# Third chunk's values first in the first batch, and squares of 32 for q and k from the sixteenth head pair

## Chip, cores and metric

The kernel runs on one core of a Trainium2 chip. The metric is device time in microseconds (us) of one launch. The kernel before was run three times: median 1395.97 us, from 1393.84 to 1398.77.

## The reference

Attention with RMS-normed queries and keys, and then a two-layer network over all heads of a token. Everything is float32 but the two weight matrices, which are handed over in float64 as pairs of 32-bit words.

```python
# q, k, v: (batch 8, heads 12, seq 448, head_dim 64); g_q, g_k: (64,)
rmsnorm(x, g) = x / sqrt(mean(x * x, axis=-1) + 1e-6) * g
scores = rmsnorm(q, g_q) @ rmsnorm(k, g_k).T / sqrt(64)
attn   = softmax(scores)                       # over the keys
x      = (attn @ v) as (8 * 448 = 3584, 768)   # heads side by side
h      = x @ w_in                              # (768, 2048)
g      = h - tanh(h)
out    = g @ w_out                             # (2048, 768)
```

## The kernel before

**Steps and slots.** Work is cut into 48 steps; step s is one batch b = s // 6 and one pair of its heads, s % 6 (NP = 6 pairs to a batch). The attention of a batch runs ahead of the network of the batch before it. The order of all instructions is written out by hand: each engine does them in the order in which the program names them, and a loop calls one function per step, a slot.

- `first_slot(s)`, s = -3 to 5: batch 0. No network work exists yet; what runs beside attention is the rounding of the float64 weights to float32 (`weight`, L290, with `round_weight_a` on ScalarE L71/L72, `round_weight_b` on VectorE L78/L82, `round_weight_c` on POOL L90) and sums of weight blocks (`combine`, L322, on VectorE).
- `early_slot(s)`, s = 6 to 11: attention of batch 1 beside the network of batch 0 (`hidden`, `project_first`), with the rest of the weights still being loaded (L265, L269) and rounded.
- `slot(s)`, s = 12 to 47: attention of batch 2 and later beside the network of the batch before. Weight blocks now come from a ring (L386, L388).

`run(gap)` (the matmuls of `stream`) puts so many ns of the network's matmuls at its place. From s = 13 (FOLDED) `slot` goes through `visit`, which mixes values and the next pair's scores.

**Attention of one pair.** The 448 keys are three chunks of 128 (c = 0, 1, 2) and a last one of 64 (KF = 3). `scores(s, c)` makes eight small matmuls (32 keys each, L506; the profile counts two instructions for each of them) and two exponentials on ScalarE (L512), into `p` for chunks 0 and 1, `p_full` for chunk 2, `p_last` for the rest. `p` and `p_last` have two buffers, `p_full` has one:

```python
name, bufs = ("p", 2) if c < 2 else ("p_full", 1) if c < KF else ("p_last", 2)
```

so the scores of pair s+1, chunk 2, can be made at once, but their exponential has to wait until the values of pair s have read `p_full`. `values(s, av)` (L598) multiplies the three chunks with v, 24 matmuls (48 instructions in the profile, L605), twelve for each half n of the queries; its loop has n outside and c inside, 0, 1, 2. `totals` (L611) sums the probabilities on TensorE and VectorE takes the reciprocal (L631); `divide` (L665) scales the values. In `first_slot` the order at the end is: the last chunk's scores of s+1, `last_values`, `values`, scores of s+1 chunk 2, `norm_q(s + 3)`, `divide`, `weight`, `combine`.

**Two ways to prepare q and k.** Pairs 0 to 17 are loaded with rows on partitions (q as 112 partitions with four rows each, k as three chunks of 128 rows with three neighbouring rows to a partition). ScalarE squares them (L123, L124), VectorE sums (L133, L134), POOL takes the power -0.5 (L135), the q rows are scaled in `norm_q` (L410, on VectorE; for pairs 9 to 14 eight ScalarE multiplications instead, the `if` at the head of `norm_q`), and `turn` (L416) transposes them on TensorE, four for k (L421), four for q (L425), with the copies to `kT` and `qT` on ScalarE (L423, L429). From pair 18 on (batch FIRST = 3), `by_blocks` is true: `load_blocks` brings q and k with eight transfers in squares of 32x32, `square_blocks` (ScalarE L451), `norm_blocks` (VectorE L458 to L462, POOL L463) and `scale_blocks` (VectorE L470) norm them, and `turn_blocks` transposes the squares on VectorE (L480, L484), with kT's scale on ScalarE (L485). No TensorE instruction is needed.

The row order of a batch has to be the same everywhere: with `turn`, the queries come out in an order that depends on how many rows a partition holds, and `store` (L822) puts them right with a strided VectorE transpose (L828) for b < FIRST, a contiguous one otherwise. For the same reason v is loaded row by row in order (`in_order` in `fetch`) for batches from FIRST.

**Queues.** All loads and stores go through SP's queue, in program order; a transfer that waits holds all behind it. The weight loads wait until POOL's L90 has freed their place. An issue also waits for the eighth transfer before it, since eight semaphores take turns.

**PSUM.** Eight banks, five "sc" and three "mm", go round in their groups; in `slot` three "sc" remain and two become `av`. A group of network products that starts (`p` 1, 5, 6 or 4 of `products`, L733) needs an "mm" bank that VectorE or ScalarE has emptied: L789 for example adds the bank of product 5 to s1.

Of the kernel before, what the change touches and what calls it, by code (L numbers as in the profile page):

```python
# [20 lines left out]
NCH = 4  # L21
# [71 lines left out]
def fetch(nc, name, t, pair, in_order=False):  # L93

    S = pair.shape[1]
    P = 128
    KF, KR = S // P, S % P
    if name == "q":
        nc.sync.dma_start(
            out=t.rearrange("p h c d -> p h (c d)"), in_=pair.rearrange("h (p c) d -> p h (c d)", c=NCH)  # L100
        )
        return
    full, rest = pair[:, : KF * P].rearrange("h (p c) d -> h p c d", c=KF), pair[:, KF * P :]
    if name == "v":
        last = t[:, :, KF]
    if in_order:
        for h in range(2):
            nc.sync.dma_start(out=t[:, h, :KF], in_=pair[h, : KF * P].rearrange("(c p) d -> p c d", p=P))
    elif name == "v":
        nc.sync.dma_start(  # L110
            out=t[:, :, :KF].rearrange("p h c d -> p h (c d)"), in_=full.rearrange("h p c d -> p h (c d)")
        )
    else:
        last = t[:, KF]
        for h in range(2):
            nc.sync.dma_start(out=t[:, :KF, h], in_=full[h])
    for r in range(2):
        nc.sync.dma_start(out=last[r * KR : (r + 1) * KR], in_=rest.rearrange("h p d -> p h d"))
# [19 lines left out]
def bounded_path(tc, ctx, q, k, v, moe_w_in, moe_w_out, out, g_col, ident, ones, half_ones, neg_half, early):  # L138
# [17 lines left out]
    nc = tc.nc  # L156
    B, H, S, D = q.shape
    DFF, DM = moe_w_out.shape
    P = 128
    CP = S // NCH  # L160
    NP = H // 2
# [7 lines left out]
    HS = S // 2  # L169
# [4 lines left out]
    BL = 32  # L174
    KF, KR = S // P, S % P
# [27 lines left out]
    def mm_bank():  # L203
        return bank_of("mm")

    loaded = {}

    def load(s, names):
        b, hp = steps[s]
        for name in names:  # L210
            src = {"q": q, "k": k, "v": v}[name]
            if s == 0 and name != "v":
                t = early[name]
            else:
                shape = [CP, 2, NCH, D] if name == "q" else [P, NCH, 2, D] if name == "k" else [P, 2, NCH, D]
                t = nat.tile(shape, F32, name=f"{name}_nat", bufs=3 if name == "v" else 2)
                fetch(nc, name, t, src[b, 2 * hp : 2 * hp + 2], by_blocks(s))
            loaded[name, s] = t


# [210 lines left out]

    FIRST, NJ = 3, S // BL

    def by_blocks(s):
        return has(s) and steps[s][0] >= FIRST

    def load_blocks(s):
# [49 lines left out]
    def sc_bank():  # L489
        return bank_of("sc")  # L490

    def scores(s, c, apart=False):

        rr, kT, qT = turned[s]
        n = S if c < KF else HS
        name, bufs = ("p", 2) if c < 2 else ("p_full", 1) if c < KF else ("p_last", 2)
        if c == 1:
            p = probs[s, 1] = probs[s, 0]
        else:
            p = probs[s, c] = pp.tile([P, 2, 2 if c < 2 else 1, n], F32, name=name, bufs=bufs)  # L500
        tiles = [sc_bank() for _ in range(2)]

        def score(h, i):
            at, first = (i * BL, 0) if c < KF else (i * BL % KR, i * BL // KR * n)
            r = slice(h * D, (h + 1) * D)
            nc.tensor.matmul(  # L506
                tiles[h][i * BL : (i + 1) * BL, :n], lhsT=kT[r, c * P + at : c * P + at + BL],
                rhs=qT[r, first : first + n], start=True, stop=True,
            )

        def exp(h):
            nc.scalar.activation(  # L512
                p[:, h, c if c < 2 else 0, :], tiles[h][:, :n], AF.Exp,
                scale=1.0 if rr is None else rr[:, 0, 2 * c + h : 2 * c + h + 1],
            )

        if apart:
            return [(lambda i, h=h: score(h, i), lambda h=h: exp(h)) for h in range(2)]
        for i in range(P // BL):
            for h in range(2):  # L520
                score(h, i)
        for h in range(2):
            exp(h)

    def full(s):

        return probs[s, 0][:, :, 0], probs[s, 1][:, :, 1], probs[s, 2][:, :, 0]
# [67 lines left out]
        if has(s + 1):  # L595
            scores(s + 1, 2)

    def values(s, av):  # L598
        v_nat, p = loaded.pop(("v", s)), full(s)
        for n in range(2):  # L600
            for c in range(KF):
                for m in range(2):
                    for h in range(2):
                        r = (2 * m + h) * BL
                        nc.tensor.matmul(  # L605
                            av[n][r : r + BL, :HS], lhsT=v_nat[:, h, c, m * BL : (m + 1) * BL],
                            rhs=p[c][:, h, n * HS : (n + 1) * HS], start=False, stop=(c == KF - 1),
                        )
        return av

    def totals(s, dn):  # L611
# [328 lines left out]
    def has(s):  # L940
        return 0 <= s < NS

    def first_slot(s):

        if has(s + 1):
            scores(s + 1, 0)
            scores(s + 1, 1)
        if has(s + 2):
            turn(s + 2, mm_bank(), sc_bank())
        if s > -3:  # L950
            load(s + 4, "qk")
        if s > -3:
            squares(s + 3)
        norm(s + 3)
        if has(s):
            totals(s, mm_bank())
        if has(s + 2):
            load(s + 2, "v")
        if has(s + 1):
            scores(s + 1, KF)  # L960
        if has(s):
            av = [mm_bank() for _ in range(2)]
            last_values(s, av)
            values(s, av)
        if has(s + 1):
            scores(s + 1, 2)
            add(s + 1)
            add_last(s + 1)
        norm_q(s + 3)
        if s == -3:  # L970
            early["g_col"]()
        if has(s):
            divide(s, av)
        weight(EARLY * (s + 3) // (NP + 2))
        combine(2)

    def early_slot(s):
        gap = gap_ns(s)
        totals(s, sc_bank())
        if has(s + 1):  # L980
            scores(s + 1, 0)
            scores(s + 1, 1)
        if has(s + 2):
            load(s + 2, "v")
        run(gap)
        if has(s + 2):
            turn(s + 2, sc_bank(), sc_bank())
        if has(s + 3):
            squares(s + 3)
        if has(s + 4):  # L990
            load(s + 4, "qk")
        run(gap)
        if has(s + 1):
            scores(s + 1, KF)
        av = [sc_bank() for _ in range(2)]
        last_values(s, av)
        divide(s, values(s, av))
        if has(s + 1):
            scores(s + 1, 2)
        for work, n in ((add, 1), (add_last, 1), (norm, 3), (norm_q, 3)):  # L1000
            run(gap / 2)
            if has(s + n):
                work(s + n)

    def slot(s):

        gap = gap_ns(s)
        av = av_banks
        if has(s + 1):
            scores(s + 1, KF)  # L1010
        if s < FOLDED:
            last_values(s, av)
            totals(s, sc_bank())
            divide(s, values(s, av))
            for c in range(KF):
                scores(s + 1, c)
        else:
            visit(s, av)
        if has(s + 2):
            load(s + 2, "v")  # L1020
        if by_blocks(s + 3):
            load_blocks(s + 3)
        blocks = by_blocks(s + 2)
        run(gap / 2)
        if has(s + 1):
            add(s + 1)
        if blocks:
            square_blocks(s + 2)
        run(gap / 2)
        if blocks:  # L1030
            norm_blocks(s + 2)
        elif has(s + 2):
            turn(s + 2, sc_bank(), sc_bank())
        ahead = has(s + 3) and not by_blocks(s + 3)
        if ahead:
            squares(s + 3)
        if has(s + 4) and not by_blocks(s + 4):
            load(s + 4, "qk")
        run(gap / 2)
        folded = has(s + 1) and s + 1 >= FOLDED  # L1040
        if has(s + 1):
            add_last(s + 1)
        if folded:
            fold(s + 1)
        run(gap / 2)
        if blocks:
            scale_blocks(s + 2)
        if ahead:
            norm(s + 3)
        if folded:  # L1050
            gather(s + 1, 0)
        run(gap / 2)
        if blocks:
            turn_blocks(s + 2, 0)
        if folded:
            gather(s + 1, 1)
        run(gap / 2)
        if blocks:
            turn_blocks(s + 2, 1)
        if ahead:  # L1060
            norm_q(s + 3)
        run(gap / 2)
        if folded:
            spread_sums(s + 1)
        run(gap / 2)
# [358 lines left out]
```

## Time and profile before

One profiled execution took 1397.86 us, 1.89 above the median of the three runs; its span, from first to last instruction, is 1396.1.

| engine | busy, us | share of span | instructions |
|---|---|---|---|
| TensorE, matmul (PE) | 1360.6 | 97% | 11864 |
| TensorE, weight load (PEld) | 1133.3 | 81% | 11864 |
| VectorE (DVE) | 940.3 | 67% | 1530 |
| ScalarE (ACT) | 507.9 | 36% | 1153 |
| GpSimd (POOL) | 555.4 | 40% | 348 |

By stage (us; the first two columns are where the stage begins and how long it lasts):

| stage | begins | length | PE busy | DVE busy | ACT busy | POOL busy | clock | DMA share |
|---|---|---|---|---|---|---|---|---|
| start, pairs prepared | 0 | 27.40 | 16.82 | 10.51 | 17.17 | 12.14 | 0.94 | 0.76 |
| batch 0, `first_slot` | 27.40 | 71.50 | 65.32 | 63.27 | 50.70 | 42.52 | 0.98 | 0.77 |
| `early_slot` | 98.90 | 197.76 | 188.16 | 163.18 | 96.24 | 95.93 | 0.97 | 0.79 |
| slots 12 to 15 | 296.66 | 110.60 | 110.60 | 72.39 | 44.51 | 39.49 | 1.00 | 0.55 |
| slots 16 to the end | 407.26 | 988.84 | 979.72 | 630.94 | 299.25 | 365.31 | 1.00 | 0.61 |

How to read it: PE is busy when a matmul runs, so 97% is an upper bound of how well it is used; the clock is the share of full speed that the chip granted TensorE; the DMA share is the mean over 16 DMA engines. The page counts 355,273 DMA packets, 250.01 MB in all (179 GB/s), of which 266,484 packets are under 512 bytes. A name such as L733 is the line of the kernel; a record "x48" is 48 instructions of one line in a row. In a slot with `turn` the page's groups show four transposes of k (273 ns each, L421) and four of q (259 ns, L425).

### The profile page before, as it was taken

What the parts mean: (1) busy time and instruction counts of PE and PEld (TensorE: products, weight loads), DVE (VectorE), ACT (ScalarE), POOL (GpSimd) and SP (SyncE); (2) the same over time, 40 slices, a digit from 0 to 9 for tenths busy, and PEclk for the clock granted to TensorE, in tenths of its full rate; (3) what the DMA queues carried; (4) which work ended last, traced back from release to release, by engine and by line L of the source; (5) the groups of instructions that cost most, each with busy time, mean ns of one, the idle gap of its engine ahead of it and who ended that gap; (6) DMA issues with size and microseconds to landing.
All of it is one profiled execution on the core that took longest, in us unless ns stands there. A gap on an engine that the chain in (4) does not pass through costs nothing.

```text
span 1396.1 us, 29929 instructions
## 1 busy us (share of the span) xinstructions
PE 1360.6 (97%) x11864; PEld 1133.3 (81%) x11864; DVE 940.3 (67%) x1530; ACT 507.9 (36%) x1153; POOL 555.4 (40%) x348
## 2 busy tenths in 40 slices
PE   6999899999999999999999999999999999999997
PEld 2468664478899898889889988988988998899997
DVE  3999888757756688567867668656885677632311
ACT  5866554234423433233332333224333243301100
POOL 4665555224432347224544245423462255402310
PEclk9999999999999999999999999999999999999999
DMA  7769788765556756666656666666556656366663
GB/s 177 175 189 245 244 253 214 207 198 166 158 142 192 182 163 182 170 155 193 181 148 176 195 156 184 184 156 176 171 166 176 172 179 192 100 189 183 192 192 89
DMA packets 355273, 250.01 MB, mean 179 GB/s; under 512 B 266484, under 2 KB 297396, under 8 KB 355124
## 3 DMA queue, kind: packets, MB, share of 16 engines
q1 hardware_dynamic: 355120, 248.00, 63.8%
q8 instruction: 96, 1.57, 0.5%
q14 instruction: 53, 0.43, 0.1%
q10 hardware_dynamic: 4, 0.00, 0.0%
HBM read 214.50 MB, written 33.42 MB: 178 GB/s over the span
## 4 chain that ended last, share of the span: by engine, by line
PE 87%; DVE 5%; DMA 3%; ACT 2%; SPq 1%; issue 1%; POOL 0%; DVEq 0%; ACTq 0%
PE mm L733 65%; PE sc L506 9%; PE sc L567 6%; PE mm L898 4%; PE sc L555 1%; DMA q_nat<-in_q_dram 1%; PE sc L605 1%; DMA w_raw<-in_moe_w_out_dram 1%; DMA w_f<-w_out 1%; DMA w_raw<-in_moe_w_in_dram 1%; DVE w_out L82 1%; PE mm L605 1%; DVE w_out L78 0%; DVE rs L631 0%; ACT p L512 0%
## 5 line engine op out<-in xcount | busy, mean ns | idle before, releaser
L733 PE MATMUL mm<-xT,w_f 128*128 128x224 f32 x1392 | 278.2, 354 | 1.4 <-DVE s L789 1.4
L733 PEld LDWEIGHTS mm<-xT,w_f 128*128 128x128 f32 x1392 | 261.3, 190 | 15.0 <-issue 10.2
L733 PEld LDWEIGHTS mm<-gT,w_f 128*128 128x128 f32 x1344 | 252.8, 190 | 12.8 <-issue 12.8
L733 PE MATMUL mm<-gT,w_f 128*128 128x224 f32 x1344 | 263.0, 354 | 0.0
L506 PE MATMUL sc<-qT,kT 64*32 64x448 f32 (+1 forms) x3072 | 219.1, 505 | 12.8 <-ACT p_last L512 9.4
L463 POOL TENSOR_TENSOR rr_mine<-rr_mine,neg_half 128x28 f32<-128x28 f32 x30 | 145.1, 4835 | 203.3 <-DVE rr_mine L462 203.3
L733 PE MATMUL mm<-tt,w_f 128*128 128x224 f32 x1044 | 208.7, 353 | 0.0
L733 PEld LDWEIGHTS mm<-tt,w_f 128*128 128x128 f32 x1044 | 197.0, 190 | 4.4 <-issue 4.4
L733 PE MATMUL mm<-tg,w_f 128*128 128x224 f32 x1008 | 197.7, 353 | 0.0
L770 POOL TENSOR_TENSOR gT<-s,th 128x448 f32<-128x448 f32 x96 | 118.6, 1245 | 188.1 <-ACT th L769 181.6
L733 PEld LDWEIGHTS mm<-tg,w_f 128*128 128x128 f32 x1008 | 190.6, 190 | 0.0
L506 PEld LDWEIGHTS sc<-qT,kT 64*32 64x32 f32 x3072 | 72.3, 107 | 84.3 <-issue 58.8
L671 DVE TENSOR_TENSOR xT<-xT,sc 128x448 f32<-128x448 f32 x35 | 21.7, 621 | 163.3 <-PE sc L506 118.5
L693 POOL TENSOR_TENSOR tt<-xT,tt 128x224 f32<-128x224 f32 x23 | 31.4, 1366 | 240.5 <-DVE xT L675 217.5
L650 ACT COPY sum_g<-sum 32x14 f32<-32x14 f32 x280 | 56.2, 201 | 180.8 <-DVE sum L642 175.0
L567 PE MATMUL sc<-p,v_nat 64*32 64x448 f32 x1120 | 110.5, 536 | 0.0
L769 ACT ACTIVATE th<-s 128x448 f32<-128x448 f32 x96 | 55.3, 576 | 114.4 <-DVE s L795 57.2
L135 POOL TENSOR_TENSOR rr<-rr,neg_half 112x8 f32<-112x8 f32 (+1 forms) x36 | 59.6, 1676 | 61.5 <-DVE rr L134 37.4
L512 ACT ACTIVATE p<-sc 128x448 f32<-128x448 f32 x120 | 65.2, 543 | 46.8 <-PE sc L506 34.5
L898 PE MATMUL mm<-gT,w_out 128*128 128x448 f32 x192 | 76.8, 556 | 0.3 <-POOL w_out L90 0.3
L898 PEld LDWEIGHTS mm<-gT,w_out 128*128 128x128 f32 x192 | 36.6, 195 | 39.3 <-issue 37.2
L567 PEld LDWEIGHTS sc<-p,v_nat 64*32 64x32 f32 x1120 | 40.6, 107 | 31.1 <-issue 31.1
(151 smaller groups left out, 1853.1 us busy)
## 6 DMA issues: line engine op xcount, KB each, us to landing
w_f<-w_in SPq DMA_DIRECT2D x196, 384.0 KB, 3.3
w_f<-w_out SPq DMA_DIRECT2D x147, 512.0 KB, 3.8
w_raw<-in_moe_w_out_dram SPq DMA_DIRECT2D x16, 768.0 KB, 5.0
out_dram<-th SPq DMA_DIRECT2D x192, 56.0 KB, 1.9
w_in<-w_out SPq DMA_DIRECT2D x21, 384.0 KB, 6.7
qk_nat<-in_q_dram SPq DMA_DIRECT2D x120, 56.0 KB, 2.3
qk_nat<-in_k_dram SPq DMA_DIRECT2D x120, 56.0 KB, 2.4
gT<-in_moe_w_in_dram SPq DMA_DIRECT2D x32, 192.0 KB, 4.2
```

The source lines that it names most:

```text
L135: nc.gpsimd.tensor_tensor(out=r, in0=r, in1=neg_half[:rows], op=ALU.pow)
L463: nc.gpsimd.tensor_tensor(out=mine, in0=mine, in1=neg_half[:, :1].to_broadcast([P, 2 * NJ]), op=ALU.pow)
L506: nc.tensor.matmul(tiles[h][i * BL : (i + 1) * BL, :n], lhsT=kT[r, c * P + at : c * P + at + BL], rhs=qT[r, first : first + n], start=True ...
L512: nc.scalar.activation(p[:, h, c if c < 2 else 0, :], tiles[h][:, :n], AF.Exp, scale=1.0 if rr is None else rr[:, 0, 2 * c + h : 2 * c + h ...
L567: nc.tensor.matmul(av[g][i * BL : (i + 1) * BL, :S], lhsT=v_nat[keys, h, c, m * BL : (m + 1) * BL], rhs=p[keys, h], start=first, stop=True ...
L605: nc.tensor.matmul(av[n][r : r + BL, :HS], lhsT=v_nat[:, h, c, m * BL : (m + 1) * BL], rhs=p[c][:, h, n * HS : (n + 1) * HS], start=False, ...
L650: nc.scalar.copy(out=acc[h * BL : (h + 1) * BL, g], in_=part[g * BL : (g + 1) * BL, h * NJ : (h + 1) * NJ])
L693: eng.tensor_tensor(out=t2, in0=x22, in1=t1, op=ALU.subtract)
L733: nc.tensor.matmul(bank[:, f * HS : (f + 1) * HS], lhsT=w[:, c * width + f, :], rhs=moving[p](c), start=(first and f == 0 and c == 0), sto ...
L769: nc.scalar.activation(th, h, AF.Tanh, bias=0.0, scale=1.0)
L770: eng.tensor_tensor(out=g[:, rows, cols], in0=h, in1=th, op=ALU.subtract)
L898: nc.tensor.matmul(bank[:, :S], lhsT=w_out_row(f, n // HC)[:, n % HC * P : (n % HC + 1) * P], rhs=g[:, f, :], start=(f == 0), stop=(f == C ...
```

## The change

Two edits. In the first batch's slots, `values` is cut in two: the values of chunk 2 for both halves of the queries come first, then chunk 2's scores of the next pair, then the values of chunks 0 and 1. `values` now has the chunk outside and the half inside wherever it is called (slots 0 to 12).

And the squares of 32 begin three pairs earlier, with pair 15 instead of 18, which is in the middle of batch 2. Since a batch can have one row order only, FIRST becomes 2: batch 2's pairs 12 to 14, which still go through `turn`, are loaded with rows in order too (`fetch` gets this for q, two transfers, and for k), v of pairs 12 to 17 is, and `store` transposes batch 2 contiguously. The eight transfers for pair 15 are issued late in slot 12, those for 16 and later at their usual place at the slot's start.

```diff
@@ fetch
     if name == "q":
+        if in_order:
+            for h in range(2):
+                nc.sync.dma_start(out=t[:, h], in_=pair[h].rearrange("(c p) d -> p c d", c=NCH))
+            return
...
     if name == "v":
         last = t[:, :, KF]
+    elif in_order:
+        last = t[:, KF]
     if in_order:
         for h in range(2):
-            nc.sync.dma_start(out=t[:, h, :KF], in_=pair[h, : KF * P].rearrange("(c p) d -> p c d", p=P))
+            to = t[:, h, :KF] if name == "v" else t[:, :KF, h]
+            nc.sync.dma_start(out=to, in_=pair[h, : KF * P].rearrange("(c p) d -> p c d", p=P))
@@ load
-                fetch(nc, name, t, src[b, 2 * hp : 2 * hp + 2], by_blocks(s))
+                fetch(nc, name, t, src[b, 2 * hp : 2 * hp + 2], in_order(s))
@@
-    FIRST, NJ = 3, S // BL
+    FIRST, NJ = 2, S // BL
+    TURNED = 2 * NP + 3
 
     def by_blocks(s):
+        return has(s) and s >= TURNED
+
+    def in_order(s):
         return has(s) and steps[s][0] >= FIRST
@@
-    def values(s, av):
-        v_nat, p = loaded.pop(("v", s)), full(s)
-        for n in range(2):
-            for c in range(KF):
+    def values(s, av, chunks=(2, 0, 1)):
+        v_nat, p = loaded["v", s], full(s)
+        for c in chunks:
+            for n in range(2):
...
-                            rhs=p[c][:, h, n * HS : (n + 1) * HS], start=False, stop=(c == KF - 1),
+                            rhs=p[c][:, h, n * HS : (n + 1) * HS], start=False, stop=(c == 1),
...
+        if 1 in chunks:
+            del loaded["v", s]
         return av
@@ first_slot
             last_values(s, av)
-            values(s, av)
+            values(s, av, (2,))
         if has(s + 1):
             scores(s + 1, 2)
+        if has(s):
+            values(s, av, (0, 1))
+        if has(s + 1):
             add(s + 1)
             add_last(s + 1)
@@ early_slot
-        if has(s + 4):
+        if has(s + 4) and not by_blocks(s + 4):
             load(s + 4, "qk")
@@ slot
-        if by_blocks(s + 3):
+        if by_blocks(s + 3) and s + 3 > TURNED:
             load_blocks(s + 3)
...
         if blocks:
             turn_blocks(s + 2, 1)
+        if s + 3 == TURNED:
+            load_blocks(s + 3)
         if ahead:
             norm_q(s + 3)
```

## The prediction

> **What bounds the kernel now.** I read the page first: its chain of waits (the first line under part 4) is TensorE almost throughout.
>
> ```profile
> PE 87%; DVE 5%; DMA 3%; ACT 2%; SPq 1%; issue 1%; POOL 0%; DVEq 0%; ACTq 0%
> ```
>
> So an edit pays only where it takes TensorE instructions away, or where TensorE waits. The change touches three stretches; I took them one at a time.
>
> First batch (about 27 to 99 us). The chain in order of time seems to say that ScalarE and TensorE take turns: the values, the third chunk's scores, then the exponential of p_full.
>
> ```profile
> 49.10 2.41 PE mm L605 x48
> 51.51 1.02 PE sc L506 x16
> 52.53 0.04 issue
> 52.57 0.71 ACT p_full L512 x2
> ```
>
> That is what the first edit attacks. But the timelines of VectorE, POOL and SP over the same slots show what the next slot really starts from (start, duration, engine; in brackets the idle time before and its releaser):
>
> ```profile
> 39.73 1.87 POOL L90 TENSOR_TENSOR w_out<-w_out,gT 128x768 int32<-128x768 int32 x1 [3.44 <-ACT n L123]
> ...
> 41.63 1.74 SPq L265 DMA_DIRECT2D gT<-in_moe_w_in_dram  x4
> 43.47 0.37 SPq L99 DMA_DIRECT2D q_nat<-in_q_dram  x1
> 43.95 1.24 SPq L116 DMA_DIRECT2D k_nat<-in_k_dram  x2
> 45.24 1.28 SPq L118 DMA_DIRECT2D k_nat<-in_k_dram  x2
> ...
> 50.13 0.63 ACT L124 ACTIVATE sq<-k_nat 128x512 f32<-128x512 f32 x1 [0.71 <-DMA k_nat<-in_k_dram]
> ...
> 50.79 0.69 DVE L133 TENSOR_REDUCE rr<-sq 128x8 f32<-128x512 f32 x1 [0.40 <-ACT sq L124]
> ```
>
> SP holds q and k behind a weight load that waits for POOL's L90 (41.60); k lands at 50.13, and only then can VectorE sum its squares. From there VectorE does not rest until 98.9; the stretches table (columns: length, busy of PE, PEld, DVE, ACT, POOL, clock, DMA share, GB/s) has
>
> ```profile
> 53.73:98.90 45.17, 41.32 (x607) 25.42 (x592) 43.93 (x61) 32.53 (x58) 28.73 (x20) 0.96 0.79 210
> ```
>
> 43.93 of 45.17 us. The first TensorE product that then runs on waits for VectorE's L789 at 98.93.
>
> Second, the early slots (99 to 297 us) have two TensorE stalls on weight transfers, 5.39 us before 170.91 and 2.50 us before 240.65. The second is read here from SP and ScalarE:
>
> ```profile
> 229.15 1.84 SPq L118 DMA_DIRECT2D v_nat<-in_v_dram  x2
> 231.04 1.12 SPq L348 DMA_DIRECT2D w_out<-w_out  x2
> 232.26 0.46 SPq L269 DMA_DIRECT2D w_raw<-in_moe_w_out_dram  x1
> ...
> 238.15 0.89 ACT L71 ACTIVATE w_out<-w_raw 128x768 f32<-128x768 f32 x1 [6.80 <-DMA w_raw<-in_moe_w_out_dram]
> ```
>
> Third, the steady slots. The stretches from one slot's end to the next, slots 15, 16, 19 and 20:
>
> ```profile
> 379.61:407.26 27.65, 27.65 (x249) 24.25 (x249) 12.95 (x20) 8.67 (x23) 6.81 (x6) 1.00 0.55 153
> 407.26:434.07 26.81, 26.81 (x241) 23.48 (x241) 17.57 (x31) 8.16 (x22) 9.00 (x5) 1.00 0.65 180
> ...
> 487.69:514.50 26.81, 26.81 (x242) 23.49 (x241) 20.73 (x34) 10.40 (x25) 11.87 (x6) 1.00 0.59 168
> 514.50:542.13 27.63, 27.34 (x242) 23.32 (x241) 23.69 (x39) 11.07 (x27) 16.10 (x10) 1.00 0.64 179
> ```
>
> Slots 12 to 15 hold eight transposes each and take 27.65; those with blocks of 32 take 26.81, but slot 20 takes 27.63.
>
> [...] the granted clock is 0.50 from 170 to 174 us and from 240 to 246, after idle times of 5.39 and also of 2.50. [...] here L480 and L484 do 128x448 in 638 and 627 ns on VectorE. [...] the page has 63.8% of 16 engines over 1396.1 us for 355120 packets, 40 ns a packet on average[...].
>
> **The change part by part.**
>
> *Third chunk first, scores behind it (slots 0 to 5).* No instruction is added. Two thirds of the values (1.6 of 2.41 us) move behind 16 score records, so p_full can start up to 1.6 us earlier; ScalarE waits 2.13, 1.14, 1.96, 2.45 and 2.97 us for it in slots 1 to 5. But k still lands at 50.13, because POOL's L90, SP's loads and VectorE before them hang on none of this, and from 50.79 VectorE is full. The later values do not hurt either: about 1.0 us later, they would be done at 43.0 and 52.4 in slots 1 and 2, before VectorE reads them at 44.47 and 53.73; in slot 5 at 84.8 against 86.49. I take 0. Bounds: +0.5, if POOL and VectorE meet less well; -2.0, since VectorE's gaps between 40 and 99 us (9.5 less 8.13, 9.5 less 8.77, and so on) are some 3 us in all, and not all can go. The same order of chunks in slots 6 to 12 changes no place of a wait: 0.
>
> *Blocks of 32 for pairs 15 to 17.* The order of instructions has 24 transposes (L421, L425) fewer on TensorE: 3 x (27.65 - 26.81) = -2.52 us. They lie on the path. ScalarE loses kT, qT and two squares (0.63 + 0.54 + 0.66 + 0.64) and gains L451 and L485 (0.95 + 0.67) per pair: hidden, it is busy under 13 of 27 us. VectorE loses 0.68 + 0.68 + 0.42 + 0.19 + 1.20 = 3.2 us and gains L458 to L462 (1.06 + 4 x 0.24 + 0.19 + 0.18), L470 (1.42) and two transposes (1.27), 5.1 us. POOL's two powers (1.67 + 1.69) become one of 4.84. VectorE is in order, and in slot 14 these land in front of L789, which empties a bank for TensorE. Slot 20 does the same work at the same place of its batch and shows the price:
>
> ```profile
> 526.55 1.11 DVE L640 STREAM_TRANSPOSE sum_T<-rows 128x896 f32<-128x896 f32 x1
> 527.70 1.08 DVE L642 TENSOR_REDUCE sum<-sum_T 128x28 f32<-128x896 f32 x1
> 528.70 0.61 DVE L789 TENSOR_TENSOR s<-mm,s 128x448 f32<-128x448 f32 x1
> ```
>
> L789 starts 14.95 us into slot 20, against 14.15 in today's slot 14 (365.36 - 351.21); TensorE waits, 27.63 - 26.81 = +0.82. Slots 19 and 21 show none, so I take it once; bounds 0 and three times (2.5). SP's eight transfers for a pair take 4.2 us (508.06 to 512.3); pair 15's stand alone late in slot 12 and pair 16's behind v's four, about 7 us, as in the steady slots, where no ring load is late for it: 0.
>
> *Rows in order for batch 2's loads.* q of pairs 12 to 14 is two transfers instead of one (896 packets of 256 B for 224), v of 12 to 17 four instead of three (768 for 256 in its main part); with pairs 15 to 17 about 12,100 packets more in all, at 40 ns over 16 engines 30 us of engine share spread over 200 us. Only one place is tight: v of pair 12 stands before the weight load at 232.26, with SP busy without a gap since 224.71. One more issue is 0.6 us, and 512 packets at 40 ns over 16 engines are at most 1.3. The stall before 240.65 grows by 0.7 in my estimate (0 to 1.9). q of pair 12 (156.45) ends before SP waits for POOL anyway: 0. The stores of batch 2 turn 128x448 in 0.65 instead of 0.93 us (L828), beside TensorE: 0.
>
> Sum: 0 - 2.52 + 0.82 + 0.7 = -1.0 us. The profiled execution took 1397.86 us (span 1396.1 and 1.8 around it), so 1396.9; it lies 1.9 above the median of the three runs, and against that median, 1395.97, I predict 1395.0.
>
> **Rivals.**
> - *The turn-taking is the true bound of the first batch.* For it: the chain's lines and 10.65 us of ScalarE waits. Against it: VectorE without a gap. If slots 1 to 5 each gave 1.2 us it would be -6.0, and with -1.0 from the rest 1389.
> - *Slower: the batch 2 loads push the early slots' weight transfers.* DMA is 0.9 to 1.0 busy in much of 108 to 300 us. If a weight load comes 2 us later at a place where TensorE has no slack, TensorE idles past 2.5 us and then runs at half clock for some 6 us as after 240.65, 3 us lost; two such places are 10 us, less 1.7 from the blocks: 1404. It decides from about 6 us of added stall. Against it: v and q are small beside the 768 KB weight loads, and one place only is tight.
> - *The blocks give nothing back.* VectorE late in slots 13, 14 and 15 alike, 3 x 0.82 = 2.5: 1396.6. Against it: slots 19 and 21 at 26.81.
> - *The change does not do what it says:* the order of instructions shows the 24 transposes gone and the scores moved, so only its effect is open.
>
> **How the numbers follow.** Forecast 0.63, first rival 0.17, second 0.12, third 0.08. No change is within 0.3%, about 4.2 us (1391.8 to 1400.2), which is what three runs that spread over 4.9 us can tell. Faster: 0.14 of the first rival and 0.04 from the forecast's low end, 0.18. Slower: 0.10 of the second and 0.02, 0.12. Same: 0.70. The bounds of the parts sum to about -4.5 and +4.9 at their ends, rarely all together; with half the runs' spread and part of the two outer rivals the range is 1389.5 to 1400. The likeliest case alone: 1392.5 to 1398.
>
> **What would show it.** Right: slots 13 and 15 at 26.81 and slot 14 at about 27.6; ScalarE's waits for p_full gone in slots 1 to 5, yet L789 still at about 98.9; the weight load of 232.26 half a microsecond later and TensorE's wait behind it near 3. Wrong: the first product well before 98 us, a third stretch of half clock between 99 and 297 us, or slots 13 to 15 above 27.7.

## The result, and the profile after

Twenty runs of each kernel: the changed one 1394.53 us at the median (1391.32 to 1395.85), the one before 1397.32 (1393.37 to 1399.12). The ratio is 0.9978, with a 95% interval from 0.9971 to 0.9984: 3.1 us less, between 2.2 and 4.1. The profiled execution took 1391.92 us (span 1390.1), one of the fastest of the twenty, so the 6.0 us by which its span is shorter than the span of before are not the gain; the steps below say which part of them is chance. The lines named from here on are 7 to 13 higher than before: L802 and L804 are the former L789 and L791, L746 the former L733, L783 the former L770, L911 the former L898, L517 the former L506, L523 the former L512, L616 the former L605, L432 the former L425, L474 and L481 the former L463 and L470, L653, L655 and L663 the former L640, L642 and L650. L71, L79 and L90 keep their numbers, and runs built on the kernel before have its line numbers, give or take two.

**First batch.** The profile's view of the tile p_full says what ScalarE waited for ahead of its exponentials there; first before (us, number of times), then after:

```profile
  PE sc L506: 10.7, 5
```

```profile
  PE sc L517: 3.5, 3
```

The edit did what it was made to do: two thirds of these waits are gone. But POOL's L90, for which SP's next loads wait (it ends at 50.38, they are issued from 50.40 on), stands where it stood (48.50 us before), VectorE is still full (43.94 of 45.17 us, 43.93 before), and TensorE takes up the network behind VectorE's L802 at the same moment. The timelines of POOL and TensorE and the stretches, after:

```profile
48.52 1.86 POOL L90 TENSOR_TENSOR w_out<-w_out,gT 128x768 int32<-128x768 int32 x1 [3.44 <-issue]
```

```profile
99.60 1.78 PE L746 MATMUL mm<-xT,w_out 128*128 128x224 f32 x8 [0.56 <-DVE s L802]
```

```profile
53.73:98.90 45.17, 39.72 (x592) 23.96 (x590) 43.94 (x61) 32.02 (x56) 28.64 (x20) 0.96 0.81 211
```

Before, this TensorE line began at 99.60 too.

**Slots 13 to 15.** The stretches from one slot's first scores to the next (length; busy of PE, PEld, DVE, ACT, POOL; clock, DMA share, GB/s), after:

```profile
314.72:341.53 26.81, 26.81 (x241) 23.48 (x240) 20.50 (x35) 11.14 (x25) 11.89 (x7) 1.00 0.62 170
341.53:369.19 27.66, 27.34 (x241) 23.32 (x241) 21.44 (x36) 11.03 (x26) 12.76 (x7) 1.00 0.69 178
369.19:396.00 26.81, 26.81 (x241) 23.48 (x241) 20.14 (x32) 8.35 (x23) 14.60 (x10) 1.00 0.61 145
```

Each took 27.65 before. Two lose 0.84, the middle one nothing, as slot 20 had shown: -1.67 us. VectorE's lines in slot 14 show the price, fold (L653, L655) in front of L802, and TensorE's lines below them who pays it:

```profile
359.11 1.11 DVE L653 STREAM_TRANSPOSE sum_T<-rows 128x896 f32<-128x896 f32 x1
360.26 1.09 DVE L655 TENSOR_REDUCE sum<-sum_T 128x28 f32<-128x896 f32 x1
361.26 0.61 DVE L802 TENSOR_TENSOR s<-mm,s 128x448 f32<-128x448 f32 x1
361.85 2.01 DVE L481 TENSOR_TENSOR qk_n<-qk_nat,rr_mine 128x896 f32<-128x896 f32 x1
363.79 0.61 DVE L804 TENSOR_TENSOR s<-mm,s 128x448 f32<-128x448 f32 x1
```

```profile
359.17 2.43 PE L746 MATMUL mm<-xT,w_f 128*128 128x224 f32 x12
361.93 5.06 PE L746 MATMUL mm<-xT,w_f 128*128 128x224 f32 x24 [0.32 <-DVE s L802]
366.83 2.43 PE L746 MATMUL mm<-tt,w_f 128*128 128x224 f32 x12
```

Where nothing waits, these products start 0.189 us apart, so the next group begins 2.27 us after twelve of them and 4.54 after twenty-four. So 0.49 us are lost ahead of 361.93, at L802, and another 0.36 within the twenty-four behind it: the starts of the single products in the trace have a pause from 364.11 to 364.45, and L804, which empties a bank there and stands behind L481 on VectorE, ends at 364.40.

**Early slots.** Here lie 4.1 of the 6.0 us. The last scores ahead of slot 12's network products start at 295.68 before and at 291.59 after, though in both profiles the products behind L802 run on at 99.60. Of the 4.1, 0.8 are there behind the first wait (5.39 us before, 5.04 after), where the following products begin at 175.45 before and at 174.65 after. The rest arises at the second wait. The TensorE timelines around 240 us, before and after:

```profile
240.65 1.74 PE L506 MATMUL sc<-qT,kT 64*32 64x448 f32 x14 [2.50 <-ACT p_last L512]
```

```profile
239.55 0.98 PE L517 MATMUL sc<-qT,kT 64*32 64x448 f32 x14 [2.16 <-ACT p_last L523]
```

The wait is a little shorter, and after it the clock (third number from the end in the stretches) is not halved. Before, then after:

```profile
243.00:245.00 2.00, 2.00 (x4) 0.95 (x3) 1.83 (x4) 0.62 (x2) 1.92 (x3) 0.50 0.72 111
```

```profile
243.00:245.00 2.00, 2.00 (x6) 0.96 (x6) 1.90 (x2) 0.00 (x0) 2.00 (x2) 1.00 0.84 187
```

This is what the experiments had to settle: whether the new loads do that, or chance.

### The profile page after: what moved, and what is told of

Its sections match the earlier page's. It is cut to its first block, busy times and chain, and to the rows that moved or that the text cites. A ratio compares the mean times of both kernels' runs of the same rounds, so it can differ in the third digit from the quotient of the medians.

```text
span 1390.1 us, 29908 instructions
## 1 busy us (share of the span) xinstructions
PE 1354.0 (97%) x11840; PEld 1127.5 (81%) x11840; DVE 940.9 (68%) x1545; ACT 505.0 (36%) x1147; POOL 561.4 (40%) x345
## 4 chain that ended last, share of the span: by engine, by line
PE 86%; DVE 7%; DMA 4%; issue 1%; SPq 1%; ACT 1%; POOL 0%; DVEq 0%; ACTq 0%
PE mm L746 65%; PE sc L517 8%; PE sc L578 6%; PE mm L911 4%; PE sc L566 1%; PE sc L616 1%; DMA w_f<-w_out 1%; DVE w_out L82 1%; DMA gT<-in_moe_w_in_dram 1%; DVE rs L644 1%; DVE w_out L79 1%; DVE w_out L331 1%; DMA k_nat<-in_k_dram 1%; DMA q_nat<-in_q_dram 1%; DVE rr L140 0%
## 5 line engine op out<-in xcount | busy, mean ns | idle before, releaser
L746 PE MATMUL mm<-xT,w_f 128*128 128x224 f32 x1392 | 278.5, 355 | 1.7 <-DVE s L802 1.7
L746 PEld LDWEIGHTS mm<-xT,w_f 128*128 128x128 f32 x1392 | 261.3, 191 | 16.0 <-issue 9.5
L746 PEld LDWEIGHTS mm<-gT,w_f 128*128 128x128 f32 x1344 | 252.8, 191 | 12.8 <-issue 12.8
L746 PE MATMUL mm<-gT,w_f 128*128 128x224 f32 x1344 | 263.0, 354 | 0.0
L474 POOL TENSOR_TENSOR rr_mine<-rr_mine,neg_half 128x28 f32<-128x28 f32 x33 | 159.7, 4840 | 218.2 <-DVE rr_mine L473 218.2
L517 PE MATMUL sc<-qT,kT 64*32 64x448 f32 (+1 forms) x3072 | 219.3, 507 | 11.8 <-ACT p_last L523 7.5
L746 PE MATMUL mm<-tt,w_f 128*128 128x224 f32 x1044 | 208.8, 353 | 0.0
L746 PEld LDWEIGHTS mm<-tt,w_f 128*128 128x128 f32 x1044 | 197.0, 191 | 4.4 <-issue 4.4
L783 POOL TENSOR_TENSOR gT<-s,th 128x448 f32<-128x448 f32 x96 | 119.9, 1257 | 196.8 <-ACT th L782 190.2
L746 PE MATMUL mm<-tg,w_f 128*128 128x224 f32 x1008 | 197.5, 353 | 0.0
L746 PEld LDWEIGHTS mm<-tg,w_f 128*128 128x128 f32 x1008 | 190.7, 191 | 0.0
L517 PEld LDWEIGHTS sc<-qT,kT 64*32 64x32 f32 x3072 | 71.8, 107 | 82.4 <-issue 57.1
L663 ACT COPY sum_g<-sum 32x14 f32<-32x14 f32 x280 | 56.2, 201 | 186.2 <-DVE sum L655 180.4
L523 ACT ACTIVATE p<-sc 128x448 f32<-128x448 f32 x132 | 71.7, 543 | 51.7 <-PE sc L517 39.1
L911 PE MATMUL mm<-gT,w_out 128*128 128x448 f32 x192 | 74.6, 544 | 0.3 <-POOL w_out L90 0.3
L911 PEld LDWEIGHTS mm<-gT,w_out 128*128 128x128 f32 x192 | 35.8, 190 | 37.2 <-issue 35.2
L142 POOL TENSOR_TENSOR rr<-rr,neg_half 112x8 f32<-112x8 f32 (+1 forms) x30 | 49.6, 1677 | 38.0 <-DVE rr L141 34.4
```

Of the source, the lines that this page charges most:

```text
L142: nc.gpsimd.tensor_tensor(out=r, in0=r, in1=neg_half[:rows], op=ALU.pow)
L474: nc.gpsimd.tensor_tensor(out=mine, in0=mine, in1=neg_half[:, :1].to_broadcast([P, 2 * NJ]), op=ALU.pow)
L517: nc.tensor.matmul(tiles[h][i * BL : (i + 1) * BL, :n], lhsT=kT[r, c * P + at : c * P + at + BL], rhs=qT[r, first : first + n], start=True ...
L523: nc.scalar.activation(p[:, h, c if c < 2 else 0, :], tiles[h][:, :n], AF.Exp, scale=1.0 if rr is None else rr[:, 0, 2 * c + h : 2 * c + h ...
L663: nc.scalar.copy(out=acc[h * BL : (h + 1) * BL, g], in_=part[g * BL : (g + 1) * BL, h * NJ : (h + 1) * NJ])
L746: nc.tensor.matmul(bank[:, f * HS : (f + 1) * HS], lhsT=w[:, c * width + f, :], rhs=moving[p](c), start=(first and f == 0 and c == 0), sto ...
```

## The experiments

### Each part alone, and the changed kernel again

`a_order` is the kernel before with the new `values` and `first_slot` only. `b_blocks` has the old order and the old loads, and only `TURNED = 2 * NP + 3` in `by_blocks`; its work is the same, but part of its output is another one. `after_again` is the changed kernel once more. `c_in_order` has the old order and FIRST = 2, with `TURNED` moved out to pair 18, so that pairs 15 to 17 still go through `turn`:

```diff
-    FIRST, NJ = 3, S // BL
+    FIRST, NJ = 2, S // BL
+    TURNED = 3 * NP
```

> The kernel before with the first edit alone (order of the chunks in values, and first_slot's split); loads, FIRST and blocks as before. VectorE-bound theory: ScalarE's wait for p_full falls from 10.7 us in all to about 3.5, POOL's L90 still at 48.5 and 95.75, first product still at 99.6, time unchanged: 0, within 0.7 us. Turn-taking rival: the first product comes at 94 to 98 us and the kernel gains 2 to 5 us. Clock rival (the small gain of the whole change over the 1.7 us of the blocks comes from the early slots' stalls, whatever edit moves them): the first product stays at 99.6 but the time falls by 1 to 1.5 us.

> The kernel before with the squares of 32 for pairs 15 to 17 alone; first_slot and chunk order as before, the loads and the store of batch 2 as before. Pairs 15 to 17 then meet v in another row order than their keys, and batch 2's output rows are put right as for the old order, so that part of the output is another one; the work is the same. My theory: slots 13 and 15 at 26.81, slot 14 at 27.66, -1.7 us; early slots as in the kernel before. Rival (the blocks also bring the early-slot gain, by taking the loads of pair 15 out of slot 11): -3 us. Rival (blocks give all back): 0.

> The kernel before with batch 2's loads and store in row order alone (FIRST = 2); pairs 15 to 17 still go through turn, with q and k loaded in order too. My theory as predicted: +0.7 us (0 to 1.9), the weight load behind v half a microsecond later and TensorE's wait at 240 us near 3. Rival (the early-slot gain in the changed kernel's profile is these loads' doing): -1 to -1.5 us, with the wait near 2.2 and no half clock after it. Rival (only chance from run to run): 0.

> The changed kernel once more, for a second profile. If the missing stretch of half clock after 240 us is a property of the change: again full clock from 240 to 247 and a wait of about 2.2 us there, and nearly all runs near 1392. If it falls out differently from run to run: some runs near 1392 and some near 1395, and the half-clock stretch in the profile when its time is near 1395. Against the kernel before -2.5 to -3.5 us.

Each ratio is to runs of the kernel before in the same session, 39 of them here, with a median of 1396.53 us.

| kernel | median, us | ratio to the kernel before (95% interval) |
|---|---|---|
| a_order | 1396.70 | 1.0002 (0.9994 to 1.0011) |
| b_blocks | 1394.91 | 0.9988 (0.9979 to 0.9998) |
| c_in_order | 1396.06 | 0.9996 (0.9987 to 1.0004) |
| after_again | 1394.27 | 0.9983 (0.9974 to 0.9991) |

The order of the chunks is worth nothing that can be measured (0.3 us slower, between 0.8 faster and 1.5 slower), the blocks 1.7 us (0.3 to 2.9), the loads something between a gain of 1.8 and a loss of 0.6. The turn-taking rival is out: in `a_order`, too, the products behind the first batch run on at 99.60. The clock can't be read from one profile: `after_again`, at 1392.57 us, had a wait of 1.88 us, shorter than 2.16, and half clock behind it, while `d_old` below, with the loads of before, waited longest and had none. The stretches of `after_again` and of `d_old`:

```profile
239.00:241.00 2.00, 2.00 (x15) 0.55 (x16) 1.97 (x4) 0.47 (x2) 1.31 (x1) 0.50 1.05 297
```

```profile
241.00:243.00 2.00, 2.00 (x18) 0.87 (x5) 1.94 (x5) 1.16 (x2) 1.75 (x1) 1.00 0.54 149
```

What can be read is the weight load itself, since nine profiles of this study leave this stretch of code alone but for the loads and, in five of them, the order of the chunks in `values` (old in `before`, `b_blocks`, `d_old` and `c_in_order`). "After v" is from the issue of the weight load before it, which precedes v, to its own issue; "flight" from its issue to the start of ScalarE's L71 on it; "half clock" is the time from the end of TensorE's wait to the scores near 294 us, less the 52.04 us that it takes where the clock stays at 1.00.

| kernel | batch 2's loads | after v | flight | TensorE waits | half clock costs |
|---|---|---|---|---|---|
| before | old | 7.55 | 5.89 | 2.50 | 2.99 |
| a_order | old | 7.25 | 6.02 | 2.35 | 2.95 |
| b_blocks | old | 7.48 | 5.49 | 2.05 | 1.65 |
| d_old | old | 7.71 | 6.04 | 2.82 | 0.00 |
| d_new | old | 7.47 | 6.19 | 2.73 | 3.04 |
| after | in order | 7.97 | 5.12 | 2.16 | 0.00 |
| after_again | in order | 7.75 | 5.05 | 1.88 | 1.52 |
| c_in_order | in order | 7.72 | 5.01 | 1.80 | 1.65 |
| f_fold | in order | 7.75 | 5.02 | 1.83 | 1.65 |

The one issue more does delay the weight load, by 0.31 us in the mean (7.49 to 7.80). But its flight is shorter by 0.88 (5.93 to 5.05), without an overlap between the two groups, so TensorE waits 0.57 less in the mean (2.49 to 1.92). It is the loads and not the order of the chunks: `c_in_order`, with the old order, has the short flight, and `a_order` and `d_new`, with the new one, the long. The half clock costs 2.1 in one group's mean and 1.2 in the other's, but single values go from 0 to 3 in the first; five and four profiles don't separate that. What the single values go with is shown in the last section.

### Is VectorE the bound of the first batch?

The first try moved the scaling of q for pairs 4, 6 and 8 to ScalarE, with the old order (`d_old`) and with the new (`d_new`):

```diff
-        if NP + 3 <= s < 2 * NP + 3:
+        if s in (4, 6, 8) or NP + 3 <= s < 2 * NP + 3:
```

> The kernel before, with the scaling of q for pairs 4, 6 and 8 on ScalarE (eight multiplications) instead of VectorE's L410: some 8 us less for VectorE and 6 more for ScalarE in the first batch. VectorE-bound theory: the first product comes 3 to 8 us before 99.6, and the kernel is faster by some of that, at least 2 us. Turn-taking rival (ScalarE with TensorE is the bound): no gain or a loss, 0 to +4 us. Third: weight transfers or POOL's L90 hold it, 0.

> The same relief of VectorE together with the new order of the first batch (no blocks, loads as before). If VectorE is the only bound, the new order adds nothing to the relief: same as the relief alone within 0.7 us. If ScalarE's turn with TensorE is the next bound behind VectorE, the new order is now worth 1 us or more over the relief alone.

Ratios 1.0004 (0.9996 to 1.0011) and 1.0003 (0.9995 to 1.0011): no gain. This was no test of VectorE. L410 takes 0.627 us in the first batch; I had put in its mean of 2.67 in slots 12 to 15, so 1.9 us were taken off VectorE and not 8. And the multiplications stand ahead of the squares on ScalarE, so that VectorE came to wait for them (its timeline in `d_old`):

```profile
51.31 0.69 DVE L133 TENSOR_REDUCE rr<-n 112x8 f32<-112x512 f32 x1 [3.50 <-ACT n L123]
```

The second try gives no engine more work. It leaves out L79, a step of the weights' rounding that takes 0.56 to 0.91 us each time on VectorE, for the eight weight pieces of the first batch, on top of `e_before` (next section). The output is then another one, and all other work is the same:

```diff
-def round_weight_b(nc, raw, dst):
+def round_weight_b(nc, raw, dst, shift=True):
...
+    if shift:
...
-                round_weight_b(nc, raws[n - 1], weight_dst(n - 1))
+                round_weight_b(nc, raws[n - 1], weight_dst(n - 1), n > EARLY)
```

> e_before without L79 (a shift of 0.56 to 0.91 us on VectorE) for the eight weight pieces rounded in the first batch: those weights keep a wrong exponent, so the network's output is another one; all other work is the same. VectorE loses some 5 us in the first batch and no engine gains any. VectorE-bound theory: L789 and the first product come 3 to 5 us before 99.6, and the kernel is as much faster than e_before. If POOL's L90, the weight transfers or ScalarE hold the first batch: 0 to -1 us.

> The same without L79, together with the new order of the first batch. If VectorE is still the bound: within 0.5 us of h_old. If with VectorE relieved the turn of ScalarE and TensorE comes next: 1 us or more faster than h_old.

`h_old` took 1384.54 us (1383.98 to 1384.88), 3.4 under `e_before` at 1387.91 (1386.85 to 1389.23). `h_new` took 1384.81 (1383.45 to 1385.65). So VectorE's work is on the path there: in the profiles, the values behind the first products (`p_last`) begin at 98.05 in `h_old` and at 101.26 in `e_before`. POOL's L90, which comes behind L79 for the same weights, moves forward with it, so the runs don't tell whether VectorE's fullness or its place ahead of POOL counts for more. The new order adds nothing that shows within the 2.2 us of `h_new`'s spread, even when some 5 us of VectorE's work are gone; single profiles have both signs, about 1.1 us for it in `d_new` against `d_old` and 1.1 against it in `h_new` against `h_old`. The stretch of `h_old` shows why there is little to win: VectorE is as full as ever.

```profile
53.73:98.90 45.17, 43.49 (x655) 26.75 (x644) 43.99 (x62) 35.27 (x63) 30.30 (x21) 1.00 0.77 205
```

### The waits of the early slots

In the early slots, ScalarE's exponential of the last chunk (`p_last`) stands behind L71, which waits for a weight transfer, and TensorE's next scores wait for that exponential's bank. ScalarE's timeline in the changed kernel, ahead of the scores at 239.55:

```profile
237.05 0.89 ACT L71 ACTIVATE w_out<-w_raw 128x768 f32<-128x768 f32 x1 [6.49 <-DMA w_raw<-in_moe_w_out_dram]
237.84 0.89 ACT L72 ACTIVATE w_raw<-w_raw 128x768 int32<-128x768 uint32 x1
238.63 0.52 ACT L917 COPY s<-mm 128x448 f32<-128x448 f32 x1
239.04 0.79 ACT L523 ACTIVATE p_last<-sc,rr 128x224 f32<-128x224 f32 x2
```

`e_early` is the changed kernel with these scores ahead of the network products that bring L71:

```diff
             turn(s + 2, sc_bank(), sc_bank())
+        if has(s + 1):
+            scores(s + 1, KF)
         if has(s + 3):
             squares(s + 3)
...
         run(gap)
-        if has(s + 1):
-            scores(s + 1, KF)
```

`e_before` has the same edit on the kernel before.

> The changed kernel, with the last chunk's scores of the next pair in the early slots put before the second stretch of network products, so that their exponential does not queue behind ScalarE's L71, which waits for a weight transfer. Theory (TensorE's waits at 165 to 170 and 237 to 240 us are ScalarE's queue, and the half clock follows from them): both waits shrink below 1 us, clock 1.0 after them, -6 to -10 us against the changed kernel, -9 to -13 against the one before. Rival (the weight transfers themselves are the bound, and the next product needs them): the waits move behind L90 or L82, 0 to -2 against the changed kernel.

> The kernel before, with the last chunk's scores of the next pair put before the second stretch of network products in the early slots, as in e_early. With the waits at 170 and 240 us and the half clock gone, it shows what the change is worth without them: e_early stands at 1385.61. If the blocks' 1.68 us are all that the change does in instruction time, this kernel is at 1387.3, within 0.3. If the rows in order cost or bring something besides, it is off by that: 1386.6 if they cost the 0.7 us predicted, 1388.5 if they or the order of chunks bring 1.2.

`e_early` took 1385.61 us (1385.3 to 1385.8): ratio 0.9919 (0.9907 to 0.9932) to the kernel before, and 8.9 us under the changed kernel's median. Both waits are gone, and so is the half clock:

```profile
98.90:200.00 101.10, 97.77 (x880) 74.11 (x882) 92.08 (x118) 60.17 (x112) 61.33 (x36) 1.00 0.81 243
200.00:281.00 81.00, 81.00 (x557) 39.40 (x552) 67.58 (x97) 32.05 (x69) 35.38 (x24) 1.00 0.85 227
```

Behind the wait for L802 at 99.8, TensorE's timeline has two smaller waits of some size left there:

```profile
186.83 1.77 PE L911 MATMUL mm<-gT,w_out 128*128 128x448 f32 x4 [1.58 <-POOL gT L783]
...
189.92 0.60 PE L432 MATMUL sc<-ident,n 112*128 112x112 f32 x4 [0.89 <-ACT p L523]
```

So what held TensorE was the exponential's place in ScalarE's queue; the transfers alone do not. The prediction had called these waits stalls on weight transfers. Most of the spread goes with them: the changed kernel's twenty runs lie 4.5 us apart, these five 0.5, the six of `e_before` 2.4.

`e_before` took 1387.91 us (1386.85 to 1389.23). The change is thus worth 2.3 us without the waits, between medians of two sessions and with 2.4 us of spread in the one kernel; in the two profiles, from the first product to the end of the span, it is 1285.45 less 1284.01, 1.4 us. The blocks' 1.67 lie between. Within that spread, no cost of the loads shows, and no gain.

### Fold out of the way

`fold` (L653, L655) stands in front of L802 in slot 14, and in slots 20, 26, 32, 38 and 44 likewise. `f_fold` puts it a quarter gap later there; `best`, on top of `e_early`, puts it behind `scale_blocks` and a quarter gap. The edit of `best`:

```diff
+        late_fold = folded and steps[s][1] == 2
-        if folded:
+        if folded and not late_fold:
             fold(s + 1)
...
             scale_blocks(s + 2)
...
+        if late_fold:
+            run(gap / 4)
+            fold(s + 1)
         if folded:
             gather(s + 1, 0)
-        run(gap / 2)
+        run(gap / 4 if late_fold else gap / 2)
```

> The changed kernel, with fold (L653, L655 on VectorE) a quarter gap later in the slots of the third pair of each batch. Theory (slots 14, 20, 26, 32, 38, 44 lose 0.85 us each because fold stands in front of L802): those slots at 26.81, -5 us against the changed kernel, -8 against the one before. Rival (something else holds L802, or the stall moves to the next use): 0 to -1 against the changed kernel.

> e_early with fold put behind scale_blocks and a quarter gap in the slots of the third pair of each batch, so that L802 and L804 both stand in front of it on VectorE. Theory (VectorE's order before L802 is all that slots 14, 20, 26, 32, 38 and 44 lose): these slots at 26.81 and 1380.5, 5.1 us under e_early. Rival (VectorE is too full there and the wait goes to the next use of a bank): 1385 to 1385.6.

`f_fold` took 1394.27 us, the changed kernel's time: a quarter gap was too little, L802 still came behind fold on VectorE, so this run tells nothing of the cause. `best` took 1407.90 (1406.86 to 1408.34), 22.3 over `e_early`, 3.7 in the mean for each of the six slots. Its slot 14 shows that L802 and L804 are early, and what came in their place (VectorE, then ScalarE, then TensorE):

```profile
352.86 0.62 DVE L802 TENSOR_TENSOR s<-mm,s 128x448 f32<-128x448 f32 x1
355.60 2.01 DVE L481 TENSOR_TENSOR qk_n<-qk_nat,rr_mine 128x896 f32<-128x896 f32 x1 [2.12 <-POOL rr_mine L474]
```

```profile
360.31 1.78 ACT L663 COPY sum_g<-sum 32x14 f32<-32x14 f32 x8 [11.08 <-DVE sum L655]
```

```profile
363.37 4.05 PE L746 MATMUL mm<-tt,w_f 128*128 128x224 f32 x12 [2.63 <-DVE gT L783]
```

VectorE's scaling, L481, has to wait for POOL's power; fold used to fill that time. Fold then ends at 360.3, ScalarE's copies of its sums wait for it, the tanh of the network waits behind the copies, L783 behind the tanh, and TensorE, after 0.57 us for L804, waits 2.63 for L783 and falls to a clock of 0.57 from 364 to 368. So the order in front of L802 is not all that these slots hang on. A place for fold between the two was not tried.

## Why the prediction was right, and where it was not

- **The sum.** 1395.0 was predicted and 1394.53 measured, but against the twenty runs of before the gain is 3.1 us and not 1.0. That the two numbers lie so close is luck: the median of three runs on which the forecast stood, 1395.97, lies 1.35 under that of the twenty, 1397.32, and this makes up for most of the gain that was missed. The forecast of no change beyond 0.3% holds (3.1 us are 0.22%), though the gain is clear of zero. The upper bound of the parts, +4.9, adds up the costs and leaves out the -2.52 of the blocks; with it, it is +2.4.
- **Third chunk first: 0, right, and for the reason given.** The wait for p_full shrank by 7.2 us and nothing followed: k waits for SP, SP for POOL, and VectorE has no gap. `a_order` measured +0.3 us (-0.8 to +1.5), and `h_old` with `h_new` show VectorE's work on the path and no gain of the new order beside it.
- **Blocks: -2.52 + 0.82, right to 0.03.** The trace has -1.67, in slots 13 and 15 and not in 14, with L802 late behind fold as forecast, and L804 late behind L481 besides; `b_blocks` measured -1.7.
- **Rows in order: +0.7, the step that failed, in its sign.** It priced the queue and not the flight. The issue is later by 0.31 where I had put 0.6; the packets in the way, for which I had allowed up to 1.3 at the mean of 40 ns a packet, did not delay the weight load: it lands 0.88 sooner after its issue. TensorE's wait was to grow from 2.50 to about 3; it is 0.57 shorter in the mean. Which neighbour makes room (v in four transfers, or the q and k behind the weight load) was not tried, and stays open.
- **What is left,** about 0.9 us of the 3.1, is within the measurement's interval; the half clock after 240 us can hold it, whose cost differs from execution to execution by up to 3 us. I had taken that stretch for a fixed cost of the wait; the changed kernel lost nothing to it in one profile and 1.52 us in the other, and in the nine profiles it goes with where the wait fell against the starts of half clock (last section). Whether a part of the 0.9 is the loads' doing is not shown.

## What to carry to other kernels

A wait in the chain that alternates between two engines is not a bound until a third engine's gaps have been looked at: here ScalarE waited 7 us less and the next stage began at the same microsecond. When a transfer moves ahead of an urgent one, its issue is only a part of the price (here 0.31 us later at the issue, and 0.88 less in flight); the time of flight has to be measured, not worked out from a packet count. A difference of one to three microseconds behind a TensorE wait should not be read from a single profile: here two profiles of one kernel lost 0 and 1.52 us to half clock behind the wait at one place. And before an instruction is taken from in front of a late one, ask what wait it covers (here 2.12 us of VectorE's for POOL, ahead of L481) and what is queued behind its reader on the other engine (here the tanh, for which TensorE in the end waited 2.63).

## What the runs showed of the hardware

The half clock did not follow the length of TensorE's wait. In the nine profiles, waits of 1.80 to 2.82 us at the same place cost 0, 1.5 to 1.65, or about 3.0 us more afterwards; the longest one cost nothing, one of 1.80 us cost 1.65.

What it went with is where the wait fell against the starts of half clock. The traces record when the granted clock changes. In the first profiles of the two kernels every stretch of half clock lasts 3.41 or 6.83 us, but for the one that the end of the execution cuts off, and they all begin a whole number of 3.413 us apart: before, at 18.14, 76.17, 168.33 and 240.01 us; after, at 16.89, 78.33 and 167.08. In the other seven, stretches of 2 us give the starts to some hundredths: each has one between 167 and 171 us, and all but `d_old` have one near 240, which comes 68.3 us later in `a_order` and 71.7 later in the rest, 20 and 21 times 3.413. Where these starts lie against the program differs from one execution to the next: `f_fold`, whose code is that of the changed kernel up to slot 12, has one at 168.64 us, the changed kernel in its two profiles at 167.08 and 167.12. The table lays windows of 3.41 us on them (for `after` and `d_old`, which have no start near 240, counted on from 167.08 and 170.72) and gives TensorE's idle time in the first window that the wait touches and in the next one.

| kernel | wait | idle in the first window | idle in the next | half clock behind the first window |
|---|---|---|---|---|
| d_new | 2.73 | 2.18 | 0.54 | 6.83 |
| before | 2.50 | 1.86 | 0.64 | 6.83 |
| a_order | 2.35 | 1.62 | 0.73 | 6.83 |
| b_blocks | 2.05 | 2.05 | 0.00 | 3.41 |
| f_fold | 1.83 | 1.83 | 0.00 | 3.41 |
| c_in_order | 1.80 | 1.80 | 0.00 | 3.41 |
| after_again | 1.88 | 1.70 | 0.18 | 3.41 |
| after | 2.16 | 1.37 | 0.79 | 0 |
| d_old | 2.82 | 1.24 | 1.58 | 0 |

In these nine, half clock came behind the windows that held 1.62 to 2.18 us of idle time, and not where the wait was split into 1.37 and 0.79 or into 1.24 and 1.58. It went on for a second window in the three where 0.54 to 0.73 of the wait fell into its first one, and not in the four where that was 0.18 or nothing. So the 3 us that the first profile of the changed kernel saves here are read as chance: its wait of 2.16 was split, and that of `d_old`, with the old loads and the longest wait, was too and cost as little. `after_again`, the same kernel with its starts within 0.05 us of the same places, had a wait that began 0.3 us earlier and held 1.70 in one window, and it lost 1.52. The windows are an ordering of these nine waits, made after the fact; what sets the starts, and whether other waits fall in line, was not shown.
